# q, k and v of five units by seven of eight block products, FFN1's sums from ScalarE copies, a bf16 layer boundary and transposes read from SBUF

## The chip, the cores and the metric

The kernel runs on one core of a Trainium2 chip. TensorE (PE) multiplies matrices into PSUM, VectorE (DVE) and ScalarE (ACT) do elementwise work, SyncE (SP) issues nearly all DMAs. The metric is the device time of one execution in microseconds (us), the median of several runs.

## The reference

Two layers, each an attention block A and a feed-forward block B, with the same weights in both. x is (1, 2048, 1024), bf16.

```python
def A(x):                       # 32 heads of 32, window W = 8, dilation 2
    q, k, v = split(x @ wqkv)   # wqkv 1024 x 3072
    # position s sees s, s-2, ..., s-14; positions below 0 are masked
    attn = softmax(q . k[window] / sqrt(32))
    return (attn . v[window]) @ wo          # wo 1024 x 1024
def B(x):
    r = relu(x @ w1 + b1)       # w1 1024 x 3584
    return (r * r) @ w2 + b2    # w2 3584 x 1024
x = x + A(layernorm(x)); x = x + B(layernorm(x))    # twice
```

## The kernel before

**Units.** Tokens are taken by parity, so that a dilation of 2 becomes a window of 8 neighbours. A block is 512 tokens of one parity (`BLK`), half a block 256 (`HB`). Four blocks times two layers are the eight units u = 0 to 7. Activations are kept transposed, with features on the partitions and tokens along the free axis: `xnA` is the normalised input of attention, `xnB` that of the feed-forward block.

**The stages of a unit.** `SA(u)` loads four tiles of 128 tokens and normalises them (`ln`): ScalarE makes the f16 tile `xn`, ScalarE's queue stores it in DRAM (`xnd`, L460), and SyncE issues a DMA transpose (L502) that reads it back into `xnA`. `SQ` multiplies by wqkv: 24 groups of eight matmuls of 512 columns (L600) fill PSUM banks `pq`, and ScalarE casts each to f16 `q`, `k` or `v` (L613). `S2` is the attention, nearly all on VectorE: products `P` of q with shifted k (L644) are summed in a tree (L652), TensorE sums them over a head's channels (`lg`, L659), ScalarE takes the exponent (L670), VectorE sums the denominators (L684 to L686), ScalarE inverts them (L689, L690), and VectorE multiplies with v (L705) and adds up to `o` (L711). It is done for half 0 of the block and then half 1. `SW` multiplies o by wo (`py`, L741); VectorE adds the input x (`xm`, L746), and a second layer norm gives `xnB` as above. `SF1` is the first feed-forward product, `SF2` the second (L917), `out_tile` (L971) adds the residual and stores to `xs` between the layers (f32) or to the output.

**Seven of eight.** From unit 1 on, FFN1 and FFN2 work by blocks: a 2 x 2 block product that takes eight block multiplications is done with seven, from sums and differences of blocks (a Strassen-like scheme). The combinations of weights are made once, in unit 0 (`keep_w1`, `keep_w2`), and stored in DRAM (`w1s`, `tw`); those of the right-hand operand are made by VectorE in every unit (`rhs_combos`, T, L440). In FFN1 (`ffn1_step`) a step has three PSUM banks X, Y and Z and seven products of eight 256-column matmuls (L859). ScalarE copies X to SBUF after products 1, 6 and 7 (`u`, L833), since later products accumulate on top of X. VectorE adds u to Y or Z from PSUM (L836) and applies bias and relu (L843); ScalarE applies relu to the last X (L875) and squares (L847). There are seven steps in a unit, and two run interleaved (`ffn1_order`).

**The order of the work.** `build` describes the operations in program order: for u from 1, `SA(u+1)`, k of u + 1, `SW(u)`, q and v of u + 1, `S2(u+1)`, `SF1(u)`, `SF2(u)`. I call this "loop u". In u = 6 `SW(7)` is put before `SF2(6)`. A planner (`Plan.schedule`) then simulates the engines with costs written in the file (`MM`, `dve`, `act`, `LAT`, `DMA_LAT`, `DMA_MBS`) and picks for each free engine the ready operation with the lowest `prio`; `nxt()` gives rising numbers in program order, and many operations have fixed small or negative numbers that put them ahead. The resulting order is emitted, and on the chip each engine and each DMA queue works in that order. Buffers come from classes of slots (`sizes`: 9 of 8 KB a partition, 14 of 4 KB and so on) with caps for each name (`caps`: six weight buffers `w`, and so on). `after` makes an operation wait for another: the x loads of `SA(u)` wait for the last v product of unit u - 2 (`gatev`).

Of the kernel before, what the change touches and what calls it, by code (L numbers as in the profile page):

```python
# [15 lines left out]
H = 32  # L16
# [11 lines left out]
OWN_LAT = {"DVE": 0.12}  # L28
# [4 lines left out]
def act(n):  # L33
    return 0.18 + n * 0.00084
# [22 lines left out]
class Plan:  # L57
# [9 lines left out]
    def add(self, eng, dur, fn, r=(), w=(), prio=0.0, after=(), mb=0.0, lat=None, name=""):  # L67
        op = Op()
        op.eng, op.dur, op.fn, op.prio, op.mb, op.name = eng, dur, fn, prio, mb, name
        op.lat = lat if lat is not None else (DMA_LAT if mb else LAT)  # L70
# [135 lines left out]
class _Kernel:  # L206
# [19 lines left out]
    def setup(self):  # L226
# [45 lines left out]
        self.xs = [tc.dram_tile([self.S, D], F32, name=f"xs{l}") for l in range(self.n_layers - 1)]  # L272
# [4 lines left out]
        self.order1 = self.ffn1_order()  # L277
        self.w1s = [tc.dram_tile([128, min(4, len(self.order1) - i), 4, 256], F16, name=f"w1s{i // 4}") for i in range(0, len(self.order1), 4)]
        self.xnd = [tc.dram_tile([self.S, D], F16, name=f"xnd{l}{h}") for l in range(self.n_layers) for h in "AB"]
# [4 lines left out]
        sizes = [("8Q", 3, 8304), ("8K", 9, 8192), ("4K", 14, 4096), ("r2", 1, KF * BLK * 2), ("2K", 8, 2048), ("1K", 7, 1024),  # L284
# [4 lines left out]
        p.caps.update(pk=2, lg=4, w=6, xt=2, P0=4, P1=4, pr=2, pb=2, dn=1, e=1, xm=6, xnA=1, xnB=1, xn=2, xo=2, q=1, k=1, v=1, o=1, r2=1, s1=1, tv=4, T=1, wl=2)  # L289
# [94 lines left out]
    def ffn1_order(self):  # L384

        out = [(0, 1), (1, 1)]
        for a in range(0, self.NDP, 2):
            steps = [d for d in (a, a + 1) if d < self.NDP]
            then = [(d, 1) for d in (a + 2, a + 3) if d < self.NDP]
            for pr in (5, 6, 2, 7):  # L390
                out += [(d, pr) for d in steps]
            out += then
            for pr in (4, 3):
                out += [(d, pr) for d in steps]
        return out

# [32 lines left out]
    def rhs_combos(self, xnT, prio, cls):  # L429

        nc, p = self.nc, self.p
        T = Buf(cls, "T", [128, 4, 2, 4, 128], F16)
# [17 lines left out]
    def ln(self, x, xv, xcells, xnT, tl, scr, key, prio, vec, on_pe=False):  # L450
# [7 lines left out]

        def f4():
            nc.scalar.dma_start(scr(), xn[:])  # L460
# [38 lines left out]
        p.add("ACT", 0.06, f4, [(xn, 0)], [key], -1e6, mb=0.26, name="lnst")  # L499

        def f5():
            nc.sync.dma_start_transpose(xnT[:, tl], scr())  # L502
        p.add("SP", 2.6, f5, [key], [(xnT, tl)], -5.0, mb=0.45, name="lnT")
# [39 lines left out]
    def load_x(self, layer, t, after=(), prio=None, tag="xt"):  # L543
        x = Buf("4K", tag, [128, self.D], F32)
        if layer == 0:
            xv = lambda: x[:].bitcast(BF)[:, 0:self.D]
            self.dma(xv, lambda: self.par_tile(self.x_par, t), (), [(x, 0)], 0.27, prio=-10.0 if prio is None else prio, after=after, name="x")
        else:
            xv = lambda: x[:]
            self.dma(xv, lambda: self.xs[layer - 1][t * 128:(t + 1) * 128, :], [(("xs", layer - 1, t), db) for db in range(2)],  # L550
                     [(x, 0)], 0.53, prio=-10.0 if prio is None else prio, after=after, name="x")
        return x, xv

    def SA(self, u):
        layer, b = divmod(u, self.NB)
        st = self.state.setdefault(u, {})
        xnT = Buf("8K", "xnA1" if u == 1 else "xnA", [128, 4, self.KD, 128], F16)
        st["xnA"] = xnT
        after = [self.state[max(u - 2, 1)].get("gatev")] if u >= 2 else ()
        for tl in range(4):  # L560
            t = b * 4 + tl
            x, xv = self.load_x(layer, t, after, tag="x0" if u == 0 else "xt", prio=20.0 if u == 1 else None)
            if u == 0:
                self.ln_first(x, xv, xnT, tl)
            else:
                self.ln(x, xv, [0], xnT, tl, lambda t=t: self.xnd[2 * layer][t * 128:(t + 1) * 128, :],
                        (("xnd", 2 * layer, t), 0), 20.0, False)

    def SQ(self, u, jobs, order=None, split=0):
# [5 lines left out]
        first = (b % self.NBC == 0)  # L575
# [3 lines left out]
        for nm in jobs:  # L579
            st[nm] = Buf("8Q", nm, [128, NCH, offs[nm] + BLK], F16)  # L580
            ws[nm] = [self.weights(self.wqkv_v[:, 4 * kh:4 * kh + 4, cols[nm]:cols[nm] + D], 8, wide=True) for kh in range(2)]
            if nm == "q":
                continue
            dst = st[nm]
            if first:
                p.add("DVE", 0.1, lambda dst=dst: nc.vector.memset(dst[:, :, 0:HALO], 0.0), (), [(dst, "h")], -50.0, name="halo0")
            else:
                src = self.state[u - 1]["halo" + nm]
                p.add("DVE", 0.18, lambda dst=dst, src=src: nc.vector.tensor_copy(dst[:, :, 0:HALO], src[:]),
                      [(src, 0)], [(dst, "h")], -50.0, name="halo")  # L590
        if order is None:
            order = [(nm, c0) for nm in jobs for c0 in range(NCH)]
        for nm, c0 in order:
# [17 lines left out]
            else:  # L611
                st["gate" + nm] = self.pe(8, fm, [(xnT, i) for i in range(4)] + [(w[0], 0), (w[1], 0)], [(pq, 0), (pq, 1)], name="pq")
            p.add("ACT", act(512), lambda dst=dst, c0=c0, off=off, pq=pq: nc.scalar.copy(dst[:, c0, off:off + BLK], pq[:]),  # L613
                  [(pq, 0), (pq, 1)], [(dst, c0)], 2.0, name="cast")
            yield
        for nm in jobs:
            if nm != "q":
                h = Buf("H", "halo", [128, NCH, HALO], F16)
                st["halo" + nm] = h
                p.add("DVE", 0.18, lambda h=h, dst=st[nm]: nc.vector.tensor_copy(h[:], dst[:, :, BLK:BLK + HALO]),  # L620
                      [(st[nm], c) for c in range(NCH)], [(h, 0)], -50.0, name="halos")

    def S2(self, u, depths):
# [10 lines left out]
        def prod(hb):  # L634
# [5 lines left out]
            for c in range(NCH):  # L640
# [5 lines left out]
                p.add("DVE", dve(2048), fp, [(q, c), (k, c), (k, "h")], [(cur, 0)], self.nxt(), name="P")  # L646
# [51 lines left out]
        def av(hb):  # L698
# [3 lines left out]
            for c in range(0, NCH, 2):  # L702
                prs = [Buf("4K", "pr", [128, W, HB], F16) for _ in range(2)]
                for pr, ch in zip(prs, (c, c + 1)):
                    p.add("DVE", dve(2048), lambda pr=pr, ch=ch: nc.vector.tensor_tensor(pr[:], pb[:], _win_ap(v[:, ch, :], HALO + hb * HB, HB), ALU.mult),  # L705
                          [(pb, 0), (v, ch), (v, "h")], [(pr, 0)], self.nxt(), name="av")
# [16 lines left out]
    def SW(self, u):  # L723
# [8 lines left out]
        for tl in range(4):  # L732
# [3 lines left out]
            for db in range(D // 512):  # L736
# [7 lines left out]
                def fe(py=py, xm=xm, xv=xv, db=db):  # L744
# [4 lines left out]
            self.ln(xm, lambda xm=xm: xm[:], [0, 1], xnT, tl, lambda t=t: self.xnd[2 * layer + 1][t * 128:(t + 1) * 128, :],  # L749
                    (("xnd", 2 * layer + 1, t), 0), 1.0, u in (0, self.NU - 1), on_pe=(u in (0, self.NU - 1)))  # L750

    def SF1_plain(self, u):
# [6 lines left out]
        for dp in range(self.NDP):  # L759
# [4 lines left out]
            for m in range(2):  # L764
                for a in range(2):
# [23 lines left out]
                    p.add("ACT", 0.69, fr, [(ph, 0), (ph, 1)], [(r, 0)], 2.0, name="relu")  # L789
                    p.add("ACT", 0.63, fs, [(r, 0)], [(r2, (f, 0)), (r2, (f, 1))], 1.9, name="sq")  # L790
# [3 lines left out]
    def SF1(self, u):  # L794
# [7 lines left out]
        T = self.rhs_combos(xnT, -60.0, "8Q" if last else "8K")  # L802
        xc = {0: [(xnT, 0), (xnT, 1)], 1: [(xnT, 2), (xnT, 3)]}

        def B(k2, n2):
            return (lambda k: xnT[:, 2 * n2:2 * n2 + 2, 4 * k2 + k, :]), xc[n2]

        def TT(i):
            return (lambda k: T[:, i, :, k, :]), [(T, (i, 0)), (T, (i, 1))]
        rhs = {1: B(0, 0), 2: B(1, 0), 3: B(1, 1), 4: TT(3), 5: TT(0), 6: TT(1), 7: TT(2)}  # L810
        steps = {}
        for j, (d, pr) in enumerate(self.order1):
            if j % 4 == 0:
                n = min(4, len(self.order1) - j)
                spare = last and j % 8 == 0
                w = Buf("8Q" if spare else "8K", "wl" if spare else "w", [128, 4, 4, 256], F16)
                self.dma(lambda w=w, n=n: w[:, 0:n], lambda j=j: self.w1s[j // 4][:],
                         [(("w1s", j // 4), i) for i in range(n)], [(w, 0)], n * 0.24, after=[st["attended"]] if spare else (), name="w")
            if d not in steps:
                steps[d] = self.ffn1_step(r2, d)  # L820
            steps[d](pr, w, j % 4, *rhs[pr])

    def ffn1_step(self, r2, dp):
# [11 lines left out]
        def vadd(r, m, i, bank):  # L835
            p.add("DVE", dve(512, False), lambda: nc.vector.tensor_tensor(r[:, :, m, :], us[i][:], bank[:], ALU.add),  # L836
                  [(us[i], 0), (bank, 0)], [(r, (a, m)) for a in range(2)], -90.0, name="hc")

        def vrelu(r, a, m, f):
# [3 lines left out]
            p.add("DVE", 0.21 + len(ms) * 0.07, lambda: nc.vector.tensor_scalar(out=v(), in0=v(), scalar1=self.b1T[:, f:f + 1], scalar2=0.0,  # L843
# [7 lines left out]
        def mul(pr, w, wi, rhs, rc):  # L851
            bank = {1: X, 6: X, 7: X, 4: X, 2: Y, 5: Z, 3: Z}[pr]
            start, raw = pr in (1, 2, 5), pr in (1, 2, 4)

            def fm():
                for a in range(2):
                    for k in range(4):
                        lw = w[:, wi].bitcast(BF) if raw else w[:, wi]
                        nc.tensor.matmul(bank[:, a, :], lw[:, k, a * 128:(a + 1) * 128], rhs(k), start=(start and k == 0 and a == 0), stop=(k == 3),  # L859
                                         skip_group_check=True)  # L860
            p.add("PE", 4 * MM, fm, rc + [(w, 0)], [(bank, 0)], self.nxt(), name="ff")
# [11 lines left out]
            elif pr == 4:  # L873
                for a in range(2):
                    p.add("ACT", 0.48, lambda a=a: nc.scalar.activation(out=r3[:, a, 0, :], in_=X[:, a, :], func=ACTF.Relu,  # L875
# [90 lines left out]
    def out_tile(self, layer, t, db, py, xm):  # L966
# [3 lines left out]
        xo = Buf("2K", "xo", [128, BLK], BF if final else F32)  # L970
# [4 lines left out]
        else:  # L975
            self.dma(lambda: self.xs[layer][t * 128:(t + 1) * 128, sl], lambda: xo[:], [(xo, 0)], [(("xs", layer, t), db)], 0.27, prio=-10.0)
# [21 lines left out]
    def build(self):  # L998
# [12 lines left out]
        for u in range(NU):  # L1011
            if u + 1 < NU:
# [6 lines left out]
                else:  # L1019
                    self.run(self.SQ(u + 1, "k"))  # L1020
                    self.SW(u)
                    self.run(self.SQ(u + 1, "q"))
# [53 lines left out]
```

## Time and profile before

| | |
|---|---|
| median of 3 runs | 1203.03 us (1202.13 to 1203.26) |
| the profiled execution | 1204.91 us, span of the trace 1203.2 us |
| granted TensorE clock | 0.999 of full speed |
| DMA | 348 MB, mean 289 GB/s; hardware queues 82.4% (SyncE) and 3.3% (ScalarE) of 16 engines |
| matmuls of q, k, v (L600) | 1512 in 331.7 us |
| FFN1 matmuls (L859), X from T alone | 1104 in 135.2 us |

Lines of the profile name an engine, a line of the kernel (L600), an operation and out<-in by the program's names with buffer numbers left out. A busy time is a union; the mean of one operation can be longer than the distance between two starts, since operations overlap at their ends. A bracket at the end of a timeline line gives the idle time before it and what released it.

### The profile page before, as it was taken

Reading aid. Unit: us, or ns where it says so; the run is one execution under the profiler, and the core shown is the slowest. Engines: PE = TensorE matmul, PEld = TensorE weight load, DVE = VectorE, ACT = ScalarE, POOL = GpSimd, SP = SyncE. Lnnn points to the kernel's source line nnn. Section 1 sums busy time; section 2 is a strip of 40 time slices with the busy share of each in tenths; the row PEclk is TensorE's granted clock in tenths of the full one; section 3 lists DMA queues with packets and bytes.
Section 4 is the critical chain, followed back from the end, with each engine's and each line's share of the span. In section 5 each row is a group of like instructions: output and inputs, shape, how many; then the busy total and the mean of one; then the engine's idle time right before and its main releaser. Section 6 shows DMA issues by size and latency. Waiting matters only on the chain.

```text
span 1203.2 us, 18058 instructions
## 1 busy us (share of the span) xinstructions
PE 1183.3 (98%) x6923; PEld 743.0 (62%) x6923; DVE 987.2 (82%) x1583; ACT 651.0 (54%) x1190; POOL 5.0 (0%) x13
## 2 busy tenths in 40 slices
PE   6999999999999999999999999999999999989998
PEld 4665544557845686456854578555784567734863
DVE  4799999639998499976999489993999849988562
ACT  4743783178902887048850698317891275711640
POOL 1000000000000000000000000000000000000000
PEclk9999999999999999999999999999999999999999
DMA  9779999869998798977989789997999875687963
GB/s 280 227 222 260 300 335 331 311 206 303 292 381 303 234 303 319 367 250 267 359 315 387 247 254 341 325 331 236 298 311 379 303 226 229 215 308 285 352 231 143
DMA packets 209222, 348.02 MB, mean 289 GB/s; under 512 B 67184, under 2 KB 134000, under 8 KB 196336
## 3 DMA queue, kind: packets, MB, share of 16 engines
q1 hardware_dynamic: 197984, 333.22, 82.4%
q10 hardware_dynamic: 7488, 13.63, 3.3%
q0 software_dynamic: 3664, 0.02, 0.4%
q8 instruction: 54, 0.88, 0.3%
q14 instruction: 32, 0.26, 0.1%
HBM read 292.30 MB, written 46.40 MB: 281 GB/s over the span
## 4 chain that ended last, share of the span: by engine, by line
PE 85%; DVE 6%; DMA 5%; ACT 2%; SPq 1%; issue 1%; ACTq 0%; DVEq 0%
PE pq L600 21%; PE X L859 13%; PE X L917 13%; PE py L741 7%; PE Z L859 7%; PE Z L917 6%; PE py L361 4%; PE ph L772 4%; PE Y L917 3%; PE Y L859 3%; DMA w<-in_B_w_dram 3%; DVE P L644 2%; PE lg L659 2%; DVE P L652 1%; DMA w<-in_A_wqkv_dram 1%; SPq L305 1%
## 5 line engine op out<-in xcount | busy, mean ns | idle before, releaser
L600 PE MATMUL pq<-xnA,w 128*128 128x512 f16 x1512 | 331.7, 379 | 1.7 <-DMA w<-in_A_wqkv_dram 1.7
L600 PEld LDWEIGHTS <-w 128*128 128x128 bf16 x1512 | 216.6, 144 | 111.4 <-DMA w<-in_A_wqkv_dram 2.1
L859 PEld LDWEIGHTS <-w 128*128 128x128 f16 (+1 forms) x2544 | 248.8, 98 | 36.2
L644 DVE TENSOR_TENSOR P<-q,k 128x2048 f16<-128x2048 f16 x128 | 152.2, 1222 | 83.8 <-ACT q L613 83.8
L917 PEld LDWEIGHTS <-r 128*128 128x128 f16 x1176 | 115.2, 98 | 144.3 <-issue 8.2
L917 PE MATMUL X<-w,r 128*128 128x512 f16 (+1 forms) x784 | 176.8, 380 | 0.9 <-DMA w<-in_B_w_dram 0.9
L613 ACT CAST k<-pq 128x512 f16<-128x512 f32 x64 | 37.5, 586 | 218.2 <-PE pq L600 183.4
L705 DVE TENSOR_TENSOR pr<-pb,v 128x2048 f16<-128x2048 f16 x128 | 153.1, 1220 | 0.2
L859 PE MATMUL X<-T,w 128*128 128x256 f16 x1104 | 135.2, 273 | 0.0
L711 DVE TENSOR_TENSOR pr<-pr 128x1024 f16<-128x1024 f16 (+1 forms) x256 | 129.0, 548 | 0.0
L652 DVE TENSOR_TENSOR P<-P,P 128x2048 f16<-128x2048 f16 x96 | 115.9, 1216 | 0.1
L741 PE MATMUL py<-w,o 128*128 128x512 bf16 x512 | 112.3, 379 | 0.0
L847 ACT ACTIVATE r<-rr 128x1024 f16<-128x1024 f16 x98 | 102.6, 1058 | 6.0 <-DVE rr L843 4.1
L833 ACT CAST u<-X 128x512 f16<-128x512 f32 x147 | 83.6, 585 | 37.7 <-PE X L859 33.2
L741 PEld LDWEIGHTS <-o 128*128 128x128 bf16 x512 | 50.0, 98 | 59.8
L746 DVE TENSOR_TENSOR xm<-py,xt 128x512 f32<-128x512 f32 x64 | 44.1, 689 | 50.3 <-PE py L741 49.1
L836 DVE TENSOR_TENSOR rr<-u,Z 128x512 f16<-128x512 f16 x98 | 65.5, 681 | 17.1 <-ACT u L833 10.4
L613 ACT CAST v<-pq 128x512 f16<-128x512 f32 x64 | 36.7, 583 | 26.9 <-PE pq L600 23.4
L843 DVE TENSOR_SCALAR rr<-rr,b1T 128x256 f16<-128x256 f16 (+1 forms) x196 | 50.2, 312 | 0.3
L917 PE MATMUL Y<-w,r 128*128 128x512 bf16 x196 | 45.4, 386 | 4.5 <-DMA w<-in_B_w_dram 4.5
L361 PE MATMUL py<-w,r 128*128 128x512 bf16 x224 | 49.7, 379 | 0.0
L875 ACT ACTIVATE rr<-X,b1T 128x256 f16<-128x256 f32 x98 | 42.8, 472 | 11.6 <-PE X L859 11.1
(112 smaller groups left out, 1260.0 us busy)
## 6 DMA issues: line engine op xcount, KB each, us to landing
w<-w1s SPq DMA_DIRECT2D x78, 1024.0 KB, 8.6
w<-tw SPq DMA_DIRECT2D x56, 896.0 KB, 8.3
w<-in_A_wqkv_dram SPq DMA_DIRECT2D x48, 1024.0 KB, 7.6
w<-in_B_w_dram SPq DMA_DIRECT2D x42, 896.0 KB, 7.0
w<-in_A_wo_dram SPq DMA_DIRECT2D x16, 1024.0 KB, 7.8
xt<-xs SPq DMA_DIRECT2D x32, 512.0 KB, 7.7
w<-in_B_w_dram SPq DMA_DIRECT2D x28, 512.0 KB, 7.6
xs<-xo SPq DMA_DIRECT2D x32, 256.0 KB, 5.9
```

The lines of the kernel that those rows point to most:

```text
L361: nc.tensor.matmul(bank[:], r2[:, k2 * h + j0 + j, tl * 128:(tl + 1) * 128], w[:, k2, j, n2 * BLK:(n2 + 1) * BLK], start=False, stop=(j0 + ...
L600: nc.tensor.matmul(pq[:], wv[:, kd % 4, c0:D:8], xnT[:, :, kd, :], start=(kd == 0), stop=(kd == KD - 1))
L613: p.add("ACT", act(512), lambda dst=dst, c0=c0, off=off, pq=pq: nc.scalar.copy(dst[:, c0, off:off + BLK], pq[:]), [(pq, 0), (pq, 1)], [(ds ...
L644: nc.vector.tensor_tensor(cur[:], q[:, c, None, hb * HB:(hb + 1) * HB].to_broadcast([128, W, HB]), _win_ap(k[:, c, :], HALO + hb * HB, HB) ...
L652: nc.vector.tensor_tensor(other[:], other[:], cur[:], ALU.add)
L705: p.add("DVE", dve(2048), lambda pr=pr, ch=ch: nc.vector.tensor_tensor(pr[:], pb[:], _win_ap(v[:, ch, :], HALO + hb * HB, HB), ALU.mult), ...
L711: nc.vector.tensor_tensor(dst, pr[:, 0:n, :], pr[:, n:2 * n, :], ALU.add)
L741: nc.tensor.matmul(py[:], o[:, c, tl * 128:(tl + 1) * 128], wos[c // 4][:].rearrange("p (a b) n -> p a (b n)", a=4)[:, c % 4, db * 512:(db ...
L833: p.add("ACT", act(512), lambda: nc.scalar.copy(us[i][:], X[:]), [(X, 0)], [(us[i], 0)], 1.0, name="u")
L847: p.add("ACT", act(1024), lambda: nc.scalar.activation(out=r2[:, f:f + 2, :].rearrange("p a t -> p (a t)"), in_=r[:].rearrange("p a m t -> ...
L859: nc.tensor.matmul(bank[:, a, :], lw[:, k, a * 128:(a + 1) * 128], rhs(k), start=(start and k == 0 and a == 0), stop=(k == 3), skip_group_ ...
L917: nc.tensor.matmul(banks[q][:], left(jj, q), w[:, j, :], start=(start and jj == 0 and b2 is None), stop=(jj == h - 1), skip_group_check=True)
```

## The change

1. **q, k and v of units 3 to 7** are computed by seven block products, like FFN1. In unit 2 (`QU`) the weights are combined and stored in DRAM (`keep_wqkv`, `wqs`); a combination of the right-hand operand xnA is made in each unit from 3 (`TA`). For each of q, k and v there are two steps, interleaved; a step takes seven products and gives chunks 2s, 2s+1, 4+2s, 5+2s. VectorE makes three of its four outputs as u + Y or u + Z, ScalarE casts the fourth. Dependencies of q, k, v become finer: by chunk and half.
2. **FFN1:** ScalarE copies Y and Z to f16 `y`; VectorE adds u and y, both in SBUF.
3. **Layer boundary:** `xs` is bf16 and x tiles are bf16 (2 KB a partition).
4. **Transposes** read `xn` in SBUF. The store to `xnd` and the DRAM tiles are gone.
5. **Planner and gates:** costs of ScalarE are lower (`act` 0.05 + 0.00084 n), its results reach itself after 0.1 and others later by 0.12; classes and caps of buffers change; `SA(u)` waits for the 41st FFN1 product of unit u - 2.

```diff
-OWN_LAT = {"DVE": 0.12}
+OWN_LAT = {"DVE": 0.12, "ACT": 0.1}
 def act(n):
-    return 0.18 + n * 0.00084
+    return 0.05 + n * 0.00084
...
-        op.lat = lat if lat is not None else (DMA_LAT if mb else LAT)
+        op.lat = lat if lat is not None else DMA_LAT if mb else LAT + (0.12 if eng == "ACT" else 0.0)
...
-        self.xs = [tc.dram_tile([self.S, D], F32, name=f"xs{l}") for l in range(self.n_layers - 1)]
+        self.xs = [tc.dram_tile([self.S, D], BF, name=f"xs{l}") for l in range(self.n_layers - 1)]
+        self.QU = 2
+        self.orderq = {"k": self.interleave([("k", 0), ("k", 1)]), "qv": self.interleave([("q", 0), ("q", 1), ("v", 0), ("v", 1)])}
...
-        sizes = [("8Q", 3, 8304), ("8K", 9, 8192), ("4K", 14, 4096), ("r2", 1, KF * BLK * 2), ("2K", 8, 2048), ("1K", 7, 1024),
+        sizes = [("8Q", 3, 8304), ("8K", 9, 8192), ("4K", 12, 4096), ("r2", 1, KF * BLK * 2), ("2K", 10, 2048), ("1K", 11, 1024),
...
+    def keep_wqkv(self, nm, ws):
...
+            for pr, m, k in ((1, 0, 0), (2, 0, 1), (4, 1, 1)):
+                t = Buf("2K", "tr", [128, 4, 256], BF)
+                p.add("ACT", act(1024), lambda t=t, m=m, k=k: nc.scalar.copy(v4(t), raw(m, k)), [(ws[k], 0)], [(t, 0)], 30.0, name="trc")
+                store(pr, t, BF)
...
+            def comb(t, a, b, op, r, pr):
+                p.add("DVE", dve(1024, False), lambda: nc.vector.tensor_tensor(v4(t), a(), b(), op), r, [(t, 0)], self.nxt(), name="tq")
+                store(pr, t)
+            comb(s1, lambda: raw(1, 0), lambda: raw(1, 1), ALU.add, [(ws[0], 0), (ws[1], 0)], 5)
...
+    def SQ7(self, u, job):
...
+        if "TA" not in st:
+            st["TA"] = self.rhs_combos(st["xnA"], 1.0, "8K", "TA")
+        self.seven(self.orderq[job], self.wqs[job], ("wqs", job), st["xnA"], st["TA"], lambda d: self.qkv_step(u, *d))
...
+    def qkv_step(self, u, nm, s):
...
+        def keep(i):
+            us[i] = Buf("1K", "u", [128, 2, HB], F16)
+            p.add("ACT", act(512), lambda: nc.scalar.copy(us[i][:], X[:]), [(X, 0)], [(us[i], 0)], 1.0, name="u")
+        def vadd(m, n2, i, bank):
+            p.add("DVE", dve(512, False), lambda: nc.vector.tensor_tensor(out(m, n2), us[i][:], bank[:], ALU.add),
+                  [(us[i], 0), (bank, 0)], cells(m, n2), -90.0, name="qa")
+        def mul(pr, w, wi, rhs, rc):
+            bank, fm = self.product(pr, w, wi, rhs, X, Y, Z)
+            self.state[u]["gate" + nm] = p.add("PE", 4 * MM, fm, rc + [(w, 0)], [(bank, 0)], self.nxt(), name="fq")
+            if pr == 1:
+                keep(1)
+            elif pr == 2:
+                vadd(0, 0, 1, Y)
+            elif pr == 6:
+                keep(2)
+            elif pr == 7:
+                keep(3)
+                vadd(1, 1, 3, Z)
+            elif pr == 4:
+                p.add("ACT", act(512), lambda: nc.scalar.copy(out(1, 0), X[:]), [(X, 0)], cells(1, 0), 2.0, name="cast")
+            elif pr == 3:
+                vadd(0, 1, 2, Z)
...
         def f5():
-            nc.sync.dma_start_transpose(xnT[:, tl], scr())
-        p.add("SP", 2.6, f5, [key], [(xnT, tl)], -5.0, mb=0.45, name="lnT")
+            nc.sync.dma_start_transpose(xnT[:, tl], xn[:])
+        p.add("SP", 2.6, f5, [(xn, 0)], [(xnT, tl)], -5.0, mb=0.45, name="lnT")
...
-        after = [self.state[max(u - 2, 1)].get("gatev")] if u >= 2 else ()
+        after = [self.state[u - 2].get("gatef") or self.state[max(u - 2, 1)].get("gatev")] if u >= 2 else ()
...
         def vadd(r, m, i, bank):                      # FFN1
-            p.add("DVE", dve(512, False), lambda: nc.vector.tensor_tensor(r[:, :, m, :], us[i][:], bank[:], ALU.add),
-                  [(us[i], 0), (bank, 0)], [(r, (a, m)) for a in range(2)], -90.0, name="hc")
+            y = Buf("1K", "y", [128, 2, HB], F16)
+            p.add("ACT", act(512), lambda: nc.scalar.copy(y[:], bank[:]), [(bank, 0)], [(y, 0)], 1.5, name="y")
+            p.add("DVE", dve(512), lambda: nc.vector.tensor_tensor(r[:, :, m, :], us[i][:], y[:], ALU.add),
+                  [(us[i], 0), (y, 0)], [(r, (a, m)) for a in range(2)], -90.0, name="hc")
...
+        st["gatef"] = self.ffs[40]
...
-                    self.run(self.SQ(u + 1, "k"))
+                    plain = u + 1 <= self.QU
+                    self.run(self.SQ(u + 1, "k")) if plain else self.SQ7(u + 1, "k")
                     self.SW(u)
-                    self.run(self.SQ(u + 1, "q"))
-                    self.run(self.SQ(u + 1, "v"))
+                    self.run(self.SQ(u + 1, "qv")) if plain else self.SQ7(u + 1, "qv")
```

Seven products of a step are, in the order in which they run, 1, 5, 6, 2, 7, 4, 3 (`interleave`); products 1, 6, 7 and 4 go to bank X, 2 to Y, 5 and 3 to Z.

## The prediction

> **What bounds the kernel now.** I began with the page's first part, which says how busy each engine is over the whole span.
>
> ```profile
> span 1203.2 us, 18058 instructions
> PE 1183.3 (98%) x6923; PEld 743.0 (62%) x6923; DVE 987.2 (82%) x1583; ACT 651.0 (54%) x1190; POOL 5.0 (0%) x13
> ```
>
> TensorE has 20 us without work in 1203. The chain that ended last gives PE 85%, DVE 6%, DMA 5%. So matmul time that is taken away can be time won, if the other engines keep up in each stage. I therefore cut one loop (u = 2, units 2 and 3) at its stages: k of the next unit, attention output (py), q and v, FFN1, FFN2. The columns are stretch, length, then busy time of PE, PEld, DVE, ACT and POOL with instruction counts, granted clock, DMA share, GB/s.
>
> ```profile
> 369.10:382.90 13.80, 13.80 (x65) 9.09 (x64) 13.80 (x24) 4.11 (x7) 0.00 (x0) 1.00 0.74 263
> 382.90:396.70 13.80, 13.80 (x66) 6.35 (x64) 6.15 (x13) 9.31 (x19) 0.00 (x0) 1.00 0.57 188
> 396.70:424.30 27.60, 27.60 (x131) 18.28 (x130) 16.11 (x21) 24.78 (x51) 0.00 (x0) 1.00 0.79 258
> 424.30:467.80 43.50, 43.50 (x389) 37.81 (x387) 42.59 (x69) 38.28 (x67) 0.00 (x0) 1.00 1.04 332
> 467.80:512.60 44.80, 44.38 (x214) 20.82 (x213) 43.48 (x69) 8.55 (x15) 0.00 (x0) 1.00 0.96 342
> ```
>
> The loop takes 143.5 us and PE is busy in all of it but 0.42. DVE is busy 13.80 + 6.15 + 16.11 + 42.59 + 43.48 = 122.1, so 21.4 us idle. Where that idle time lies is shown by VectorE's timeline.
>
> ```profile
> 396.76 0.69 DVE L746 TENSOR_TENSOR xm<-py,xt 128x512 f32<-128x512 f32 x1 [1.03 <-PE py L741]
> 408.88 3.51 DVE L644 TENSOR_TENSOR P<-q,k 128x2048 f16<-128x2048 f16 x3 [11.43 <-ACT q L613]
> ...
> 527.20 0.48 DVE L711 TENSOR_TENSOR o<-pr 128x256 bf16<-128x256 f16 x2
> 528.21 0.69 DVE L746 TENSOR_TENSOR xm<-py,xt 128x512 f32<-128x512 f32 x1 [0.53 <-PE py L741]
> ```
>
> Attention starts at 408.9 and runs almost without a gap to 527.6. Its second half is needed by the third token tile of py, 526.4 + 6.9 = 533.3. That is the second chain: it has 5.7 us to spare in a loop. It starts 12.2 us after q's first matmul (396.6) because of ScalarE, which works in order and finishes the layer norms first:
>
> ```profile
> 406.61 1.24 ACT L457 ACTIVATE xn<-xm,sm 128x1024 f16<-128x1024 f32 x1
> 407.88 0.34 ACTq L460 DMA_DIRECT2D xnd0B<-xn  x1
> 408.26 4.01 ACT L613 CAST q<-pq 128x512 f16<-128x512 f32 x8 [0.41 <-ACT xn L457]
> ```
>
> **The change, part by part.** *TensorE.* The prices are in the chain (start, length, what) and the groups (count, busy us, mean ns of one):
>
> ```profile
> 291.00 3.49 PE X L859 x32
> 369.09 13.81 PE pq L600 x64
> ...
> L836 DVE TENSOR_TENSOR rr<-u,Z 128x512 f16<-128x512 f16 x98 | 65.5, 681 | 17.1 <-ACT u L833 10.4 <-PE Z L859 6.6
> L833 ACT CAST u<-X 128x512 f16<-128x512 f32 x147 | 83.6, 585 | 37.7 <-PE X L859 33.2 <-ACT xn L457 2.5 <-DVE o L711 0.3
> L440 DVE TENSOR_TENSOR T<-xnB 128x512 f16<-128x512 f16 x28 | 10.7, 419 | 0.1
> ```
>
> A 512-column matmul costs 13.81 / 64 = 0.2158 us, a 256-column one 3.49 / 32 = 0.1091. Per unit, q, k and v are 24 x 8 = 192 of the first, 41.4 us; by seven products they are 6 steps x 7 x 8 = 336 of the second, 36.65. That is 4.8 us a unit and **23.9 us for units 3 to 7**, all on the path. Weight loads stay hidden: FFN1 has the same shape already, with PE busy throughout.
>
> *VectorE, per loop.* Added: 18 sums from PSUM, the row L836. Back to back two of them took 1.28 us, so 0.60 each: 10.8. The eight right-hand combinations of xnA are the row L440, two in 0.75, so 0.335 each: 2.7. Removed: in FFN1 21 sums read f16 copies in SBUF instead of PSUM, the shape of L440, 0.60 to 0.335: 5.6. Net +7.9, 130.0 in a loop that PE would do in 143.5 - 4.8 = 138.7. It fits on the average, so what counts is the attention chain. After q starts it gains 3.6 of v sums, 3.6 of k sums and 2.7 of combinations, all of which the planner puts before attention, and loses 5.6: +4.3. Its deadline comes earlier by the 1.6 us of k and the 3.2 of q and v, 4.8 in all. The 5.7 to spare become -3.4 if attention starts 12.2 us after q again. But the first q half is complete after 7 products, 6.1 us, plus a copy and a sum, 7.5 us; if ScalarE lets those copies in between the layer norms (the planner now has a lag of 0.1 us after a ScalarE operation, which lets others in), the chain starts 4.7 earlier and has 1.3 to spare. So 0 to 3.4 us a loop. PE can also do q products before the late py tiles. I take 1.25, for four loops (u = 2 to 5) **+5**.
>
> *Writing the combinations, once, in unit 2.* 24 VectorE operations, 1024 elements, with a stride of 8 elements. Nothing in the trace has this stride. [...] The cover is there in loop u = 1:
>
> ```profile
> 227.37 2.47 DVE L971 TENSOR_TENSOR xo<-py,xm 128x512 f32<-128x512 f32 x4
> 240.61 0.18 DVE L620 COPY halo<-k 128x56 f16<-128x56 f16 x1 [10.77 <-ACT k L613]
> ...
> 265.94 3.51 DVE L644 TENSOR_TENSOR P<-q,k 128x2048 f16<-128x2048 f16 x3 [11.43 <-ACT q L613]
> ```
>
> VectorE idles 10.8 us during k, eight times 1 us in py and 11.4 before q: 30. The k operations need only the weights, so they fit the first hole; those of v come late. Behind them waits attention of unit 2. 0 to 7 us, I take **+2**. ScalarE's 18 copies (1058 ns for 1024 elements, L847: 19 us) have the lowest priority; they hold weight buffers, which I include in that range.
>
> *ScalarE.* In q, k, v 24 casts become 18 copies and 6 casts of the same size: nothing. In FFN1 21 copies of Y and Z are new: two casts in a row start 0.48 apart, 10.1 us a unit. A step then needs 6 copies (2.9), two relu (0.8) and two squares (1.95) = 5.65 us, against PE's 56 x 0.1091 = 6.1. Seven steps 39.5, with eight exps (four took 2.07) and four softmax steps (L689, L690, 0.42) 45, in an FFN1 that lasts 46 with its logits (42.8 and 16 matmuls of 0.2158). That is full. What makes it possible is that the next unit's layer norm, 19 us that lie in v and FFN1 now, is gated to the 41st FFN1 product and falls into FFN2, where ScalarE is busy 8.6 of 44.8. Behind a late copy waits the product that accumulates on the same bank X. Bounds 0 and 2.5 us a unit (the last squares then end that much later; now FFN2's first products already fill in for 6 us). I take 0.4 for seven units: **+3**. [...]
>
> *DMA.* From the packet records: 2 KB packets took 94 ns, 8 KB 335, 4 KB 176, 1 KB 50, on 16 engines. Weights for units 3 to 7: 30 MB in 2 KB packets (90 us of all engines) become 52.5 in 8 KB (141). Stores in unit 2: 42 of 256 KB, 32. Away: 52 normalised tiles to DRAM, 40; half of the boundary, 32. Net +11 on 86% of 1203: still below 90%. In loop u = 1 the stores come on top of 0.89, nearly full; the same share (1.04 to 1.10) held for 140 us in unit 0 and PE waited 0.84 us. Transposes that read SBUF are not in the trace; those from DRAM landed in 3.4 to 7.2 us (medians), the store ahead of them in 3.7 to 7.7. The step is moved off a DRAM round trip; SP waited 200 us for those stores, with weight loads queued behind. That could gain a little, or cost as much if a source in SBUF is slower: 0, bounds -4 and +4. [...]
>
> **Sum.** The profiled execution took 1204.9 us (span 1203.2 and 1.7 around it), 1.9 over the median 1203.03. 1204.9 - 23.9 + 5 + 2 + 3 = 1191.0, less 1.9: **1189**.
>
> **Rivals.** *All of it is kept* (no stall; the round trips add a little): 1203 - 24 = 1179, down to 1173 if some of PE's 20 us idle go as well, such as 5.4 us waiting for w2 loads near 1050. For: DVE's average load. Chance 0.17.
> *ScalarE becomes FFN1's bound:* its 45 us grow by waits to 2.5 us over PE, seven times 17.5, and with the 7 above it leaves about 1203: from 1197 to 1206. For: 98% load. Against: the layer norms moved out. 0.12.
> *VectorE becomes the loop's bound and the kernel slower:* its idle time per loop would have to stay over 143.5 - 130.0 = 13.5 us. [...] For: attention is already without a gap, in-order queues, and 98.5% full. Against: PE can do q before the late py tiles. 0.24.
> *The forecast*, 1182 to 1197: 0.47.
>
> **Chances and range.** 0.2% (2.4 us) is what a measurement of this kernel can tell from no change. Faster: 0.47 + 0.17 and a quarter of ScalarE's case, 0.67. Same: 0.08. Slower: 0.25. The range, 1174 to 1220, leaves out a tenth on either side.
>
> **What would show it.** Right: loops of 139 to 141 us, PE busy throughout, VectorE idle under 10 us a loop, P starting under 10 us after q's first product, ScalarE over 95% in FFN1 and some 30 us busier in FFN2. Wrong: PE waiting on u or y (ScalarE) inside FFN1; py or q products waiting for VectorE; w waiting for DMA in loop u = 1; loops over 143.

## The result, and the profile after

The changed kernel takes 1206.88 us (1205.6 to 1209.29), beside 1203.22 for the kernel before in the same runs: ratio 1.0032, 95% interval 1.0021 to 1.0043. It is slower by a little, where 1189 was forecast. The page's first part, after:

```profile
span 1204.5 us, 19912 instructions
PE 1165.5 (97%) x7594; PEld 772.9 (64%) x7643; DVE 1061.0 (88%) x1737; ACT 742.5 (62%) x1355; POOL 5.0 (0%) x13
```

TensorE is busy 18 us less, but the span is not shorter: its idle time has doubled, from 20 to 39 us. To see where, I cut the span where each unit's last FFN2 product ends. First the kernel before, loops u = 1 and u = 2 (stretch, length, busy time of PE, PEld, DVE, ACT, POOL with counts, clock, DMA share, GB/s):

```profile
226.20:369.10 142.90, 142.90 (x857) 92.52 (x856) 110.94 (x177) 84.73 (x157) 0.00 (x0) 1.00 0.87 299
369.10:512.60 143.50, 143.07 (x857) 92.35 (x856) 122.13 (x192) 85.03 (x157) 0.00 (x0) 1.00 0.89 300
```

Then the changed kernel, loops u = 1 to 5:

```profile
228.70:393.20 164.50, 149.11 (x854) 94.97 (x858) 155.94 (x213) 116.36 (x190) 0.00 (x0) 0.95 0.86 285
393.20:531.90 138.70, 138.04 (x997) 97.86 (x1001) 130.13 (x221) 93.72 (x178) 0.00 (x0) 1.00 0.91 316
531.90:671.40 139.50, 137.98 (x995) 97.69 (x1000) 128.94 (x221) 93.52 (x178) 0.00 (x0) 1.00 0.91 324
671.40:811.10 139.70, 138.25 (x996) 97.70 (x1001) 129.39 (x220) 93.62 (x178) 0.00 (x0) 1.00 0.90 313
811.10:950.00 138.90, 138.05 (x996) 97.89 (x1001) 129.33 (x222) 93.84 (x178) 0.00 (x0) 1.00 0.90 322
```

Loops u = 2 to 5 do what was forecast: 138.7 to 139.7 us in place of 142.9 to 143.5, together 16 us less. The part after loop 5 is 6.6 us shorter (254.5 for 261.1). Unit 0 ends 2.5 us later. And loop u = 1, which prepares the weights, is 21.6 us longer than before. 2.5 + 21.6 - 16.2 - 6.6 = +1.3 us, the difference of the spans (1204.5 and 1203.2). So the main question is loop u = 1. Its VectorE work has grown by 45 us. The groups say what is in it (count, busy us, mean ns of one):

```profile
L419 ACT COPY tr<-w 128x1024 bf16<-128x1024 bf16 x18 | 37.2, 2112 | 33.2 <-DMA w<-in_A_wqkv_dram 18.8 <-DMA tw<-tv 8.1 <-issue 6.4
L424 DVE TENSOR_TENSOR tv<-w 128x1024 f16<-128x1024 bf16 x12 | 24.5, 2073 | 0.0
L424 DVE TENSOR_TENSOR tv<-tv,w 128x1024 f16<-128x1024 f16 x6 | 12.5, 2084 | 0.0
L424 DVE TENSOR_TENSOR tv<-w,tv 128x1024 f16<-128x1024 bf16 x6 | 12.5, 2081 | 0.2 <-DMA wqqv<-tr 0.2
```

A combination takes 2.08 us, not the 1.14 of the prediction, and a copy 2.11, not 1.06: 49.5 us of VectorE and 37.2 of ScalarE. VectorE's timeline in that loop shows them inside the attention of unit 2, and TensorE's shows who pays:

```profile
275.17 3.60 DVE L773 TENSOR_TENSOR P<-q,k 128x2048 f16<-128x2048 f16 x3
278.59 4.18 DVE L424 TENSOR_TENSOR tv<-w 128x1024 f16<-128x1024 bf16 x2
...
291.51 2.05 DVE L424 TENSOR_TENSOR tv<-w,tv 128x1024 f16<-128x1024 bf16 x1
293.40 0.82 DVE L566 TENSOR_TENSOR T<-xnB 128x512 f16<-128x512 f16 x2
...
293.95 3.60 PE L519 MATMUL Z<-T,w 128*128 128x256 f16 x16 [4.18 <-DVE T L566]
...
314.99 1.04 PE L788 MATMUL lg<-P,grp 128*128 128x512 f16 x2 [7.55 <-DVE P L781]
```

Attention's products and the combinations T of FFN1's input stand behind the weight combinations in VectorE's order. TensorE, which also works in order, waits 4.2 us for T and 7.6 us for the P of the first logits. Of the 21.6 us, 15.4 are TensorE idle (164.5 - 149.1). The other 6 are a TensorE that is busy longer with the same work (149.1 for 142.9 us): in the stretch with these two waits its granted clock was 0.80 (third number from the end).

```profile
287.80:330.00 42.20, 30.47 (x224) 24.10 (x222) 40.72 (x53) 26.60 (x45) 0.00 (x0) 0.80 0.84 311
```

### The profile page after: what moved, and what is told of

The parts are those of the page before. It is cut to its first block, busy times and chain, and to the rows that moved or that the text cites. A ratio compares the mean times of both kernels' runs of the same rounds, so it can differ in the third digit from the quotient of the medians.

```text
span 1204.5 us, 19912 instructions
## 1 busy us (share of the span) xinstructions
PE 1165.5 (97%) x7594; PEld 772.9 (64%) x7643; DVE 1061.0 (88%) x1737; ACT 742.5 (62%) x1355; POOL 5.0 (0%) x13
## 4 chain that ended last, share of the span: by engine, by line
PE 70%; DVE 5%; DMA 3%; issue 1%; ACT 0%; SPq 0%; DVEq 0%
PE X L519 20%; PE X L1022 14%; PE Z L519 11%; PE py L870 7%; PE Z L1022 7%; PE Y L519 5%; PE Y L1022 4%; DVE tv L424 1%; DVE P L773 1%; PE lg L788 1%; DMA w<-in_B_w_dram 1%; DMA w<-in_A_wo_dram 1%; DMA xt<-in_A_x_dram 1%; DVE P L781 1%; DVE T L566 0%
## 5 line engine op out<-in xcount | busy, mean ns | idle before, releaser
L519 PEld LDWEIGHTS <-w 128*128 128x128 f16 (+1 forms) x4224 | 415.4, 98 | 70.5 <-DVE T L566 6.8
L486 ACT CAST u<-X 128x512 f16<-128x512 f32 x90 | 52.1, 579 | 119.7 <-PE X L519 119.7
L710 PE MATMUL pq<-xnA,w 128*128 128x512 f16 x552 | 122.6, 380 | 3.3 <-DMA w<-in_A_wqkv_dram 1.7
L944 ACT CAST u<-X 128x512 f16<-128x512 f32 x147 | 87.4, 616 | 46.2 <-PE X L519 39.6
L960 ACT ACTIVATE r<-rr 128x1024 f16<-128x1024 f16 x98 | 106.2, 1107 | 2.2 <-DVE rr L956 1.9
L710 PEld LDWEIGHTS <-w 128*128 128x128 bf16 x552 | 78.8, 144 | 43.2 <-DMA w<-in_A_wqkv_dram 2.1
L519 PE MATMUL X<-TA,w 128*128 128x256 f16 x720 | 86.8, 273 | 0.0
L949 DVE TENSOR_TENSOR rr<-u,y 128x512 f16<-128x512 f16 x147 | 60.2, 424 | 25.0 <-ACT y L948 20.3
L948 ACT CAST y<-Z 128x512 f16<-128x512 f32 x98 | 61.0, 641 | 10.6 <-PE Z L519 10.5
L419 ACT COPY tr<-w 128x1024 bf16<-128x1024 bf16 x18 | 37.2, 2112 | 33.2 <-DMA w<-in_A_wqkv_dram 18.8
L519 PE MATMUL Z<-T,w 128*128 128x256 f16 x352 | 44.5, 280 | 5.9 <-DVE T L566 5.9
```

What stands on the lines that cost most here:

```text
L710: nc.tensor.matmul(pq[:], wv[:, kd % 4, c0:D:8], xnT[:, :, kd, :], start=(kd == 0), stop=(kd == KD - 1))
L944: p.add("ACT", act(512), lambda: nc.scalar.copy(us[i][:], X[:]), [(X, 0)], [(us[i], 0)], 1.0, name="u")
L948: p.add("ACT", act(512), lambda: nc.scalar.copy(y[:], bank[:]), [(bank, 0)], [(y, 0)], 1.5, name="y")
L949: p.add("DVE", dve(512), lambda: nc.vector.tensor_tensor(r[:, :, m, :], us[i][:], y[:], ALU.add), [(us[i], 0), (y, 0)], [(r, (a, m)) for a ...
L960: p.add("ACT", act(1024), lambda: nc.scalar.activation(out=r2[:, f:f + 2, :].rearrange("p a t -> p (a t)"), in_=r[:].rearrange("p a m t -> ...
```

## The experiments

All are compared with the kernel before in the same runs. Loops are those of each kernel's one profiled execution.

**e1: neighbouring columns.** In `keep_wqkv`, `raw` takes a block of neighbouring columns.

```diff
-.rearrange("p a (n c) -> p a c n", c=8)[:, :, 4 * m + 2 * s:4 * m + 2 * s + 2, :]
+.rearrange("p a (c n) -> p a c n", c=8)[:, :, 4 * m + 2 * s:4 * m + 2 * s + 2, :]
```

> The changed kernel with one edit: the 24 VectorE combinations and 18 ScalarE copies of unit 2's weights read 256 neighbouring columns instead of every eighth one (q, k, v of units 3 to 7 are then those of other columns). Planner costs and so the order stay the same. Theory (the operations that read with a stride of 8 elements take 2.06 and 2.10 us instead of the planned 1.14 and 0.91, and that is what lengthens loop u = 1 from 143 to 164 us): each combination falls to 0.7 to 1.2 us, each copy to about 1.05, the loop to 140 to 146 us, the median to 1180 to 1188. Rival (the 42 stores of 256 KB and the weight loads crowd the DMA queues of that loop): the loop stays at 158 us or more, the median above 1200. Second rival (the order of work in that loop is bad whatever the durations): the same.

Measured: 1182.01 us, ratio 0.9835 (0.9804 to 0.9866). Loop u = 1 takes 142.9 us, at a granted clock of 1.00. The theory holds; the stores, the weight loads and the order of work are the same as in the changed kernel, so they are not the cause by themselves. The groups of e1, of which the second was 24.5 us before:

```profile
L419 ACT COPY tr<-w 128x1024 bf16<-128x1024 bf16 x18 | 18.4, 1057 | 38.9 <-DMA w<-in_A_wqkv_dram 37.1 <-DVE tv L336 1.8
L424 DVE TENSOR_TENSOR tv<-w 128x1024 f16<-128x1024 bf16 x12 | 8.0, 687 | 0.0
```

**e2: no seven products in q, k, v.** `QU = 99`, and `keep_wqkv` is not called.

> The changed kernel with q, k and v of all units by eight products as before, and no combinations of wqkv: the FFN1 copies, the bf16 boundary, the SBUF transposes, the gates and planner costs alone. Theory (these parts cost and bring little; the loss is in preparing unit 2's weights): loops of 143 to 144 us everywhere, u = 1 too, median 1198 to 1206. Rival (ScalarE full in FFN1 or the SBUF transposes cost time): loops over 145, median above 1210.

Measured: 1199.62 us, ratio 0.996 (0.9945 to 0.9975). Loops u = 1 to 5 take 142.9 to 144.0, as before; the part behind them is 5.5 us shorter. The other four parts together cost nothing and bring some 5 us at the end. There, in loop u = 6, TensorE waits 5.4 us for loads of w2 (`w<-in_B_w_dram`, near 1046 and 1056 us) in the kernel before, and 0.5 us in e2; which of the four parts takes that wait away was not tried.

**e5 and e6: which of the two engines.** On top of e1, so with short reads, each copy is done twice (e5) or each combination three times (e6).

```diff
-lambda t=t, m=m, k=k: nc.scalar.copy(v4(t), raw(m, k))
+lambda t=t, m=m, k=k: [nc.scalar.copy(v4(t), raw(m, k)) for _ in range(2)]       # e5
-lambda: nc.vector.tensor_tensor(v4(t), a(), b(), op)
+lambda: [nc.vector.tensor_tensor(v4(t), a(), b(), op) for _ in range(3)]         # e6
```

> The kernel of the first experiment (neighbouring columns, same order of work), with each of ScalarE's 18 copies done twice, so that a copy again takes 2.1 us while VectorE's combinations stay at 0.69. Theory (VectorE's combinations hold TensorE, ScalarE's copies hardly do): loop u = 1 at 143 to 147 us, median 1182 to 1187. Rival (the copies carry half the loss, since casts and layer norms queue behind them): loop at 150 or more, median 1190 or more.

> The kernel of the first experiment with each of VectorE's 24 combinations done three times, so that one takes 3 x 0.6 = 1.8 to 2.0 us again while ScalarE's copies stay at 1.06. Theory: loop u = 1 back at 155 to 163 us, median 1195 to 1204. Rival (it takes both, or the copies): under 150, median under 1190.

Measured: e5 1192.25 us (0.9883 to 0.9913), loop u = 1 151.0. e6 1203.88 us (0.999 to 1.0025), loop u = 1 163.9. VectorE's combinations alone bring the loss of that loop back. But my expectation for the copies was wrong: they alone cost 8 us in that loop. TensorE waits 4.4 us there, which the profile puts down to the stores of the copies, and VectorE's combinations wait 8.6 us for these stores:

```profile
L424 DVE TENSOR_TENSOR tv<-w,tv 128x1024 f16<-128x1024 bf16 x6 | 4.2, 692 | 11.5 <-DMA wqqv<-tr 8.6 <-DMA wqk<-tv 2.8
```

The two losses overlap (8 and 21 do not add up to more than 21).

**e7: the planner knows the true costs.** `comb` is planned at 1.95 for 1.14 us, the copies at 2.05 for 0.91.

> The changed kernel with strided reads, full computation; only the planner's costs of the combinations (1.95 for 1.14 us) and of the copies (2.05 for 0.91) are set to what the chip takes. Theory (it is real work, 24 x 0.8 = 19 us more VectorE time than planned in a loop whose VectorE was full): the planner can move it but not remove it, loop u = 1 at 152 to 162 us, median 1194 to 1205. Rival (the loss is the wrong order that comes from wrong costs): loop under 149, median under 1190.

Measured: 1196.35 us, 0.9927 (0.9908 to 0.9947). Loop u = 1 falls to 143.5, and loop u = 2 rises from 138.7 to 150.8. The combinations still run in loop u = 1 (219 to 298 us); what slips into loop u = 2 is attention of unit 2. VectorE's busy time there rises from 130.1 to 149.6 us, and TensorE waits 8.0 us for attention's products P. I had the place wrong and the total about right. Of the 25 us between the changed kernel and e1, a right cost in the planner gives back some 10. That the rest is work, which no order could hide, is argued and not shown: no other order was tried with these durations.

**e4: ScalarE does the strided part.** It copies all four blocks (24 copies); VectorE combines the copies, which are contiguous.

> The changed kernel, full computation; ScalarE copies all four blocks of each half (24 strided copies instead of 18, planned at 2.05 us), and VectorE's 24 combinations read those copies, contiguous f16 or bf16, planned at 0.61 us. Theory (VectorE's 24 x 2.06 us in loop u = 1 are what holds TensorE): VectorE gives back 24 x 1.4 = 33 us, ScalarE takes 6 x 2.1 = 13 more, the loop falls to 142 to 150 us, the median to 1182 to 1192. Rival (ScalarE's copies are as much to blame): the loop stays above 155, median above 1197.

Measured: 1194.03 us, 0.9919 (0.9891 to 0.9946); 148.0 in loop u = 1, 145.0 in loop u = 2. This is 2 us slower than I expected. The 24 copies at 2.11 us are 50 us of ScalarE; TensorE waits 1.8 us for ScalarE's u in loop u = 1, and in loop u = 2 2.5 us for combined weights of k and 1.5 us for TA. That the long copies cause these waits is likely and not shown.

**e3: pairs of neighbours.** The combined weights are kept as (n, c) with c of 2, and TensorE loads every second column (`lw[:, k, a::2]`). Combinations and copies then read and write two neighbours at a time.

> [...] Rival 1 (any stride costs the same): combinations stay at 2 us, median about 1206. Rival 2: the strided weight loads take 144 ns as in the plain q, k, v, and units 3 to 7 lose 1680 x 35 ns = 59 us: about 1240.

Measured: 1192.64 us, 0.9893 (0.9864 to 0.9922); loop u = 1 148.5, loop u = 2 142.1. A combination took 1.11 us and a copy 1.16, where the changed kernel has 2.08 and 2.11, and TensorE's weight loads with a stride of 2 took 98 ns as without: neither rival came. The time is 10.6 us over e1: TensorE still waits 4.1 us for P in loop u = 1, and 3.1 us for a load of wo in loop u = 2.

```profile
L419 ACT COPY tr<-w 128x1024 bf16<-128x1024 bf16 x18 | 20.1, 1155 | 39.7 <-DMA w<-in_A_wqkv_dram 25.1 <-DMA tw<-tv 9.2 <-issue 5.4
L424 DVE TENSOR_TENSOR tv<-w 128x1024 f16<-128x1024 bf16 x12 | 13.0, 1106 | 0.0
```

**e8 and e9: four neighbours.** A tile holds half of the contraction rows of both steps, so that four columns stay together; the weight loads take every fourth column. e8 has planner costs of 0.69 and 1.0 us for the combinations and copies, e9 those of the changed kernel.

```diff
-.rearrange("p a (n c) -> p a c n", c=8)[:, :, 4 * m + 2 * s:4 * m + 2 * s + 2, :]
+.rearrange("p a (n c) -> p a n c", c=8)[:, 2 * s:2 * s + 2, :, 4 * m:4 * m + 4]
-lw[:, k, a * 128:(a + 1) * 128]                                  # w[:, wi]
+lw.rearrange("p (k b) n -> p k (b n)", k=2)[:, k % 2, 2 * s + a::4]   # w[:, wi - s + k // 2]
```

> The changed kernel, full computation, with the combined weights stored so that four neighbouring columns stay together (a tile holds half of the contraction rows of both steps instead of all rows of one), planned at 0.69 and 1.0 us; TensorE's weight loads of q, k, v take every fourth column. [...] Rival: weight loads with a stride of 4 columns take longer than the 109 ns of their matmul (144 ns at a stride of 8), units 3 to 7 lose up to 59 us: 1200 to 1240.

> The kernel with runs of four neighbouring columns, full computation, with the changed kernel's planner costs (1.14 and 0.91) instead of 0.69 and 1.0, so that the order of work is that of the changed kernel and of the first experiment. Theory (with durations of 0.69 and 1.06 the old order has the room that the combinations' buffers and stores need; the tighter plan made VectorE wait 8 us for stores): loop u = 1 at 142 to 145 us, units 3 to 7 as fast as with contiguous weights although their weight loads take 113 ns for 98, median 1180 to 1186. Rival (the stores or the weight loads with a stride cost the 7 us): 1187 or more.

Measured: e8 1189.27 us, 0.9871 (0.9852 to 0.9891), loop u = 1 149.8. e9 1184.54 us, 0.9838 (0.9818 to 0.9858), loop u = 1 142.9, loops u = 2 to 5 138.7 to 139.7. e8 is below the 1200 of its rival, e9 within the range that I gave. The operations take the same in both (a combination 0.69 and 0.68 us, a copy 1.06, a weight load 104 ns in the mean), so the 7 us between them in that loop come from the order. In e8 TensorE waits 3.1 us for P and 1.7 us for T; in e9 it is idle 0.3 us in that loop. That VectorE's waits for stores are the reason, as I expected of e9, is not shown: between 200 and 300 us VectorE is idle 16.7 us in e8, of it 10.1 for stores of the new weights, but in e9 too 17.2 us, of it 5.7. e9 computes everything and is faster than both kernels. Loops u = 1 and u = 2 of e9:

```profile
227.50:370.40 142.90, 142.64 (x852) 92.48 (x856) 123.99 (x211) 104.16 (x190) 0.00 (x0) 1.00 0.97 327
370.40:509.10 138.70, 138.04 (x995) 101.68 (x1000) 130.10 (x220) 93.73 (x178) 0.00 (x0) 1.00 0.91 315
```

**e10, e11, e12: three other parts undone, each on e9.** e10 gives FFN1's sums back to VectorE from PSUM, without `y`. e11 puts the old gate (`gatev`) back. e12 stores the normalised tile in DRAM from ScalarE's queue and transposes it from there.

> The kernel of e9 with FFN1's sums read from PSUM by VectorE again, without ScalarE's copies y. Theory of the prediction (VectorE has the late chain; 21 x 0.265 = 5.6 us a loop more on it, 1 to 5 us of it visible; ScalarE's relief is worth 3 us at most over all): loops u = 2 to 5 at 140 to 145 us, median 1184 to 1200, slower than e9 by 2 to 18 us. Rival (ScalarE was the tighter one in FFN1): equal or faster than e9, by up to 5 us.

> The kernel of e9 with the x loads of the unit after next gated to v as before, so that its layer norm, 19 us of ScalarE, can fall into v and FFN1 beside the new copies. Theory (ScalarE has 45 us of its own in FFN1's 46; 19 more do not fit, but their low priority lets them slip past): loops 139 to 144 us, median 0 to 15 us over e9. Rival (the gate does nothing): within 2 us of e9.

> The kernel of e9 with the normalised tiles stored in DRAM and transposed from there as before. Prediction: a round trip off the path, worth 0 with bounds of 4 us either way: median -4 to +4 us against e9, transposes landing in 3 to 8 us. Rival (the round trip held weight loads on SyncE's queue and the late chain): over 5 us slower than e9.

Measured: e10 1197.47 us (0.9931 to 0.9969), 12.9 over e9, with loops of 144.2 for 139.7 us in u = 4 and 168.4 for 163.4 in u = 6: the ScalarE copies are worth 13 us. TensorE waits there for VectorE (4.8 us in u = 4, 7.9 in u = 6; in e9 1.1 and none). e11 1194.24 (0.9905 to 0.9934), 9.7 over e9, most of it in loop u = 1, which takes 152.6 us and so lies outside my range. There TensorE waits 3.6 us for u and 2.9 us for a load of w2. e12 1200.15 (0.9958 to 1.0011), 15.6 over e9: outside my bounds, and the rival's "over 5 us" instead; loops u = 1, 3 and 5 take 148.8, 146.8 and 143.2. TensorE's longest waits in e12 are for the combinations of xnA, which need the transposes; in loop u = 1 it is the one wait of 3.6 us for T:

```profile
PE Z L524 <- DVE TA L571: 10.8, 5, 3.3
...
PE Z L524 <- DVE T L571: 3.6, 1, 3.6
```

In e9 there is no wait for TA in that list. The issues (median us to landing) show that the transpose itself changed little; the store ahead of it is what e12 adds. First e12, then e9:

```profile
xnd<-xn ACTq DMA_DIRECT2D x52, 256.0 KB, 6.5
xnA<-xnd SPq DMA_TRANSPOSE x28, 7.7
xnB<-xnd SPq DMA_TRANSPOSE x24, 6.6
```

```profile
xnA<-xn SPq DMA_TRANSPOSE x28, 6.8
xnB<-xn SPq DMA_TRANSPOSE x24, 5.2
```

## Why the prediction was wrong, step by step

**The step that failed** is "Writing the combinations, once, in unit 2". The cost of a combination was mis-sized: 1.14 us was taken, the planner's `dve(1024, False)`, and 2.08 measured. No run shows the 1.14, on which the sum's +2 rests: it was my estimate, near the upper of two rows of the trace of before with this element count.

```profile
L684 DVE TENSOR_TENSOR dn<-e 128x1024 f32<-128x1024 bf16 x16 | 19.5, 1217 | 0.0
...
L422 DVE TENSOR_TENSOR tv<-w 128x1024 f16<-128x1024 bf16 x14 | 9.1, 679 | 0.1
```

The work was 49.5 us and not 27 (24 x 1.14), so it did not fit the 30 us of holes that were to hide it, and the term was not +2, at most 7, but 21.6. (49.5 less 30 is 19.5, not far from it.) Both rows above are contiguous. The upper one has the price of f32 results whose elements lie side by side; e1 shows that here the place of the elements sets the price (0.69 us for neighbouring columns, 2.08 for every eighth), and no row of the trace of before with this element count has VectorE reading scattered ones. One row did hint at it: the weight loads of `pq`, which read the same weights at the same stride, took 144 ns where contiguous ones took 98. I had both weight load rows and used neither. I also gave ScalarE's copies their contiguous price and let low priority hide them; e5 shows that at twice that price they cost 8 us by themselves. (The DMA share of 0.89 that the prediction gives for loop u = 1 is that of loop u = 2; loop u = 1 has 0.87.)

**TensorE's gain** was right: 4.8 us a unit forecast; loops u = 2 to 5 gained 4.8, 3.8, 3.5 and 4.0, where what is missing from 4.8 is mostly idle time of TensorE (below). The part with unit 7 gained 6.6: 4.8, and 1.8 from shorter waits for loads of w2 there (3.6 for 5.4 us).

**VectorE's late chain** was right in kind, and in size within 2 us: 5 us taken for four loops, 19.2 - 16.2 = 3.0 measured. In these loops TensorE waits 2.6 us for VectorE (1.75 for T, which comes at the end of that chain, 0.9 for sums of q and v) and 0.5 us for a load of wo, but not for `o`. VectorE has 129 to 130 us of work in 139, as computed (130.0). Attention does end late, and TensorE does q products ahead of the late py tiles:

```profile
543.96 7.07 PE L870 MATMUL py<-w,o 128*128 128x512 bf16 x31
550.87 1.91 PE L519 MATMUL X<-xnA,w 128*128 128x256 f16 x16
552.61 1.04 PE L519 MATMUL Z<-TA,w 128*128 128x256 f16 x8
553.49 7.07 PE L870 MATMUL py<-w,o 128*128 128x512 bf16 x31
```

This is loop u = 3: the second half of `o` was ready at 552.3, and the 2.6 us before it were filled. That was the argument against the slower rival, and it held. The rival needed VectorE to be idle for over 13.5 us a loop; in loops u = 2 to 5 it is idle 8.6, 10.6, 10.3 and 9.6 us. The whole range, 1174 to 1220, did contain the 1206.88, but mostly by luck: the loss lies in loop u = 1, where the combinations that push unit 2's attention late were taken at 7 us at most, and 21.6 were measured.

**ScalarE in FFN1** (+3 taken): it is full there (19.94 and 19.84 us busy in the 20 us slices from 600 and 620), but TensorE waited 0.2 us for FFN1's u over the whole kernel, so the +3 is not seen. The part takes 53 us more of engine time (the copies y 90.6 us of ScalarE, the sums 60.2 us of VectorE for 97.7); yet undoing it cost 13 us, as the engine that it frees is the one that TensorE waits for in e10.

**SBUF transposes** (0, bounds of 4 us): mis-sized, as e12 shows on top of e9. The transposes land hardly sooner than from DRAM, 6.8 and 5.2 for 7.7 and 6.6 us, but the store ahead of them, 6.5 us, is gone. In the kernel before it was hidden: TensorE waited 0.2 us for xnA in all. In the new one VectorE must combine xnA before the first products that use TA, and without the shorter way TensorE waits 10.8 us for TA. e12 also has another order of work, so how much of its 15.6 us is the latency and how much the order stays open. The DMA total was about right: the packets took 86.5% of 1203 us on all engines before and 87.1% of 1205 after, 8 us more where 11 were forecast; the new loops u = 2 to 5 have 0.90 to 0.91.

**With the failed step repaired** (e9) the kernel takes 1184.5 us, 19.8 less than the kernel before in the same runs, where the sum without that step's +2 has 23.9 - 5 - 3 = 15.9. The chain cost 2 us less and ScalarE's copies 3 us less than the sum had. But the sum compared each part with the kernel before, where the copies y and the transposes looked like +3 and 0; beside the seven products they are worth 13 and 15.6 us, which nothing in the prediction says.

## What to carry to other kernels

Price an operation by its access pattern before its element count: with every eighth two-byte element, no contiguous row of the trace bounded the price (2.08 us here, for 0.69 and 1.22 in the rows); with two neighbours kept together a combination cost 1.11 us, with four 0.69, no more than a contiguous one. Work that is done "once" must fit the slack of the one loop in which it is done, on every engine that works in order (here 49.5 us of VectorE for 30 of slack), and its cost in the planner changes what is queued behind it; the true cost helped in e7 (1196.35 for 1206.88 us) and hurt in e8 (1189.27 for 1184.54 in e9). When a change adds a consumer to a latency that was hidden (here, combinations of a transposed tile: TensorE waited 0.2 us for xnA before, and 10.8 for TA in e12), price that latency again.

## What was not expected of the hardware

- Time against neighbours kept together, for 1024 two-byte elements: VectorE tensor_tensor 2.08, 1.11, 0.69, 0.69 us for 1, 2, 4 and contiguous; ScalarE copy 2.11, 1.16, 1.06, 1.06.
- TensorE's weight loads of 128 columns: 98 ns contiguous and at every second column, 113 at every fourth (the mean of 4224 loads in e9 is 104, of which 2544 are contiguous), 144 at every eighth. At 113 ns they did not slow 256-column products that come every 109: loop u = 2 takes 138.7 us in e9 and e1 alike.
- Around waits of 4.2 and 7.6 us inside FFN1 the granted clock was 0.80 over 42 us; in e1, without these waits, it was 1.00 in that loop. That loop grew by 21.6 us, 40% more than its 15.4 of idle time.
